# A Fourier mixer and a gated MLP in one kernel: who issues the first loads, and where z1's differences are kept

## The chip, the cores and the metric

The kernel runs on one core of a Trainium2 chip. The metric is the device time of one execution in microseconds (us). Each engine has a queue of its own that it works off in order: TensorE (PE) for matrix products, VectorE (DVE), ScalarE (ACT), GpSimd (POOL), and SyncE (SP), which here only issues DMA transfers. ACT and POOL can issue transfers too; such an issue, with whatever it waits for, stands in the engine's queue like any other instruction.

## The reference

```python
mod = (silu(c) @ w_mod).reshape(...)           # sa, ca, ga, sb, cb, gb
h = layernorm(x) * (1 + ca) + sa               # x: 2048 x 512, float32
a, b = h @ hid_re.T, h @ hid_im.T              # Fourier transform over 512 columns
x = x + ga * (seq_re @ a - seq_im @ b)         # and over 2048 rows, real part
h = layernorm(x) * (1 + cb) + sb
z = gelu(h @ w_in)                             # w_in: 512 x 1792
z1, z2 = z[:, :896], layernorm(z[:, 896:])
g = w_sp @ z2 + b_sp[:, None]                  # w_sp: 2048 x 2048
out = x + gb * ((z1 * g) @ w_out)
```

All of it is float32.

## The kernel before

Every product is made of three products of a shorter format. A matrix is split in a high part, which ScalarE makes by a copy into float32r, and a low part, which DVE makes as the difference (`split`). PE then adds high x high, high x low and low x high into the same bank of PSUM.

The program is written in one order by hand: a loop runs over steps n, each with its matrix products, and a table, filled by `at(n, function, arguments)`, says what else is issued at step n. No scheduler moves anything; every engine gets its instructions in the order in which the code calls them. Waits between engines are semaphores that the framework sets. A transfer issued by SP or ACT also gets one of eight semaphore lanes, DMAHW0 to DMAHW7, in turn by the order of the code, whichever of the two engines issues it, and it waits on its own engine's queue until the transfer before it on that lane has landed.

The first part (steps 0 to N2 - 1) forms the product of the sequence transform with the normalised x. The left operand's rows, 128 at a time, are x's (`hh` and `hl`, high and low part); the right operand comes from blocks of the transform's matrix: a block (`stage`) is loaded, turned in squares of 32 by DVE (`t`, L190), and split in `ah` (ACT, L289) and `al` (DVE, L307). The products of the first four steps use the same form (`mm_a`, L501): for a row s first `ah` with `hh`, then `al` with `hh`, then `ah` with `hl`.

Before the loop stands the head, code that brings the first four rows of x in by hand. `load_two` and `load_x` load a row of x in four transfers, `load_half` half of a stage in four. `stats_first` takes a row's mean and variance on DVE and the scale and shift from them on POOL (L427, L428). `hi_first` makes hh of a row straight from x on ACT (L444) and then writes ones into its first column (L446). `norm_x` makes the normalised row `xn` on ACT, after POOL has written its first column (L468); `hi_h` makes hh from xn (L477); `lo_h` makes hl from xn and hh on DVE (L482). `prep_hi` and `prep_lo` make t and ah, and al. `keep_busy` is eight products at the very start whose result nobody uses.

The second place is z1 = gelu(h @ w_in[:, :896]), from step N2 on, at about 455 us. It is computed by a scheme of seven products in place of eight (Strassen's, in Winograd's form; the products have numbers p, in the order of `YPROD`), which needs sums and differences of quarters of h and of w_in. For it DVE forms `vj`'s low part (`lo_v`) after ACT formed its high part (`hi_v`); the halves' differences `XD`, the sums `s` (L245) and, for the columns that do not fit the scheme (product `f7`), the high and low parts of the second halves of h (`make_x`, `xh` and `xl`). ACT empties the banks: z1o (L731, a gelu) and z1p (L759, a copy back into PSUM).

```python
YPROD = (1, 2, 6, 7, 4, 5, 3)
```

Of the kernel before, what the change touches and what calls it, by code (L numbers as in the profile page):

```python
# [8 lines left out]
F32 = mybir.dt.float32  # L9
F32R = mybir.dt.float32r  # L10
AF = mybir.ActivationFunctionType
ALU = mybir.AluOpType

P = 128
# [5 lines left out]
def fnet_gmlp_kernel(  # L20
# [32 lines left out]
    nc = tc.nc  # L53
    S, D = x.shape[1:]
    F2 = w_in.shape[1]
    FH = F2 // 2
    Q = 512
# [5 lines left out]
    x = x.rearrange("b s d -> (b s) d")  # L63
# [59 lines left out]
    def at(n, f, *a):  # L123
        fill.setdefault(n, []).append((f, a))
# [9 lines left out]
    src = []  # L134
# [4 lines left out]
    N2 = 4 * len(src)  # L139
    YPROD = (1, 2, 6, 7, 4, 5, 3)  # L140
# [9 lines left out]
    stage, T, AH, AL = {}, {}, {}, {}  # L150
# [6 lines left out]
    def load_half(tile_, a, h, engs=(nc.sync,) * 4):  # L157

        v = a.rearrange("(b j) (a s) -> a j b s", j=32, a=4)
        for q in range(4):  # L160
            engs[q].dma_start(tile_[32 * q:32 * q + 32], v[q][:, :, 64 * h:64 * h + 64])
# [39 lines left out]
    def slot(i, name, dtype=F32):  # L201
        return slots[0].tile([P, Q], dtype, tag=f"slot{i}", bufs=1, name=name)

    slots, TT, S2, XH = [], {}, {}, {}

    def load_t(g):
        for k in range(ND):
            TT[k, g] = slot(1 + 4 * (g - 2) + k, f"tt{g}_{k}")
            nc.sync.dma_start(TT[k, g], ht_d[g][k * P:(k + 1) * P, :])

    def make_x(gg):

        if gg:
            XH[gg] = [[bpool[0].tile([P, Q], F32R, tag=m, bufs=3, name=f"x{m}{kk}") for m in ("bh", "bl")] for kk in range(2)]
        else:
            XH[gg] = [(slot(9 + kk, f"xh{gg}{kk}", F32R), slot(11 + kk, f"xl{gg}{kk}", F32R)) for kk in range(2)]
        for kk, (h, _) in enumerate(XH[gg]):
            nc.scalar.activation(h, TT[kk, 2 + gg], AF.Copy)
        for kk, (h, l) in enumerate(XH[gg]):
            t = TT[kk, 2 + gg]  # L220
            nc.vector.tensor_tensor(l, t, h.bitcast(F32), op=ALU.subtract)
            if not gg:
                nc.vector.tensor_tensor(t, TT[kk, gg], t, op=ALU.subtract)
        if gg:
            for kk in range(2):
                TT[kk, 3] = XD[kk]

    XD = []

    def make_d():  # L230

        for kk in range(2):
            XD.append(bpool[0].tile([P, Q], F32, tag=("bh", "bl")[kk], bufs=3, name=f"xd{kk}"))
            nc.vector.tensor_tensor(XD[kk], TT[kk, 1], TT[kk, 3], op=ALU.subtract)

    def form_t(n):

        stage1 = n < N3
        p = (YPROD if stage1 else ZPROD)[(n - (N2 if stage1 else N3)) // 4]
        gg, kk = divmod(n % 4, 2)  # L240
        a, b, c, d = TT[kk, gg], TT[2 + kk, gg], TT.get((kk, 2 + gg)), TT.get((2 + kk, 2 + gg))
        if p == 6:
            if stage1:
                S2[gg, kk] = slot(13 + 2 * gg + kk, f"s2_{gg}{kk}")
                nc.vector.tensor_tensor(S2[gg, kk], d, XD[kk] if gg else c, op=ALU.subtract)  # L245
            return S2[gg, kk]
        if stage1:
            return {1: a, 2: b, 7: a, 4: b, 5: c, 3: d}[p]
        if p in (1, 2):
            t = blocks.tile([P, Q], F32, tag="t", bufs=2, name=f"t{n}")  # L250
            nc.vector.tensor_tensor(t, a if p == 1 else b, S2[gg, kk], op=ALU.subtract if p == 1 else ALU.add)
            return t
        return {7: c, 4: d, 5: a, 3: b}[p]
# [60 lines left out]
    spool = s1.enter_context(pool("spool", "right"))  # L314
# [91 lines left out]
    def load_x(g, ks=range(4), eng=nc.sync):  # L406

        if g not in XG:
            XG[g] = spool.tile([P, 4, D], F32, tag="x", bufs=2, name=f"x{g}")
        k0, k1 = ks[0], ks[-1] + 1  # L410
        v = x.rearrange("(g a k i) d -> g a i k d", g=NQ, a=4, i=32)
        for a in range(4):
            eng.dma_start(XG[g][32 * a:32 * a + 32, k0:k1, :], v[g, a][:, k0:k1, :])
        for k in ks:
            X[4 * g + k] = XG[g][:, k, :]
# [4 lines left out]
    def stats_first(s):  # L420

        m = spool.tile([P, 12], F32, tag="first", bufs=4, name=f"first{s}")
        nc.vector.bn_stats(m[:, :6], X[s])
        mv = m[:, 8:]
        nc.vector.bn_aggr(mv[:, :2], m[:, :6])
        nc.vector.tensor_scalar(mv[:, 1:2], mv[:, 1:2], EPS, None, op0=ALU.add)
        nc.gpsimd.tensor_tensor(mv[:, 2:3], mv[:, 1:2], mhalf, op=ALU.pow)  # L427
        nc.gpsimd.tensor_scalar(mv[:, 3:4], mv[:, 0:1], mv[:, 2:3], -1.0, op0=ALU.mult, op1=ALU.mult)  # L428
        NRM[s] = mv[:, 2:3], mv[:, 3:4]
# [1 line left out]
    two = (nc.sync, nc.sync, nc.scalar, nc.scalar)  # L431

    def load_two(k):
        if not k:
            XG[0] = spool.tile([P, 4, D], F32, tag="x", bufs=2, name="x0")
        v = x.rearrange("(g a k i) d -> g a i k d", g=NQ, a=4, i=32)
        for a in range(4):
            two[a].dma_start(XG[0][32 * a:32 * a + 32, k, :], v[0, a][:, k, :])
        X[k] = XG[0][:, k, :]

    def hi_first(s):
        h_hi[s] = hpool.tile([P, ND, P], F32R, name=f"hh{s}")
        h = h_hi[s].rearrange("p k (a i) -> p k a i", i=32)
        nc.scalar.activation(h, X[s].rearrange("p (a k i) -> p k a i", a=4, i=32), AF.Identity,  # L444
                             bias=NRM[s][1], scale=NRM[s][0])
        nc.scalar.activation(h_hi[s][:, 0, :1], ones[:, :1], AF.Copy)  # L446
# [16 lines left out]
    def norm_x(s):  # L463

        if s not in LN:
            LN[s] = spool.tile([P, D], F32, tag="xn", bufs=4, name=f"xn{s}")
        if s > 1:
            nc.gpsimd.memset(LN[s][:, 0:1], 1.0)  # L468
        apply(LN[s][:, 1:], X.pop(s)[:, 1:], NRM.pop(s))
# [5 lines left out]
    def hi_h(s):  # L475
        h_hi[s] = hpool.tile([P, ND, P], F32R, name=f"hh{s}")
        nc.scalar.activation(*parts_h(s, h_hi), AF.Copy)  # L477

    def lo_h(s):
        h_lo[s] = hpool.tile([P, ND, P], F32R, name=f"hl{s}")  # L480
        lo, h = parts_h(s, h_lo)
        nc.vector.tensor_tensor(lo, h, parts_h(s, h_hi)[0].bitcast(F32), op=ALU.subtract)  # L482
        LN.pop(s)
# [172 lines left out]
    def hi_v(p):  # L656
        WJ[1, p] = wpool[0].tile([P, 2, 2, Q], F32R, tag="wj", bufs=2, name=f"vj{p}")
        nc.scalar.activation(WJ[1, p][:, 0, :, :FM], v_of(p), AF.Copy)
# [56 lines left out]
    def end_f7(g):  # L715
        end_z1(g, NF - 1, ZT.pop(("f7", g)), out_row(g, NF - 1))
# [23 lines left out]
    def mm_z1(n):  # L740
        p = YPROD[(n - N2) // 4]
        gg = n % 4 // 2
        fresh = p in (1, 5)
        a = [(AH.pop(m), AL.pop(m)) for m in (n, n + 1)]
        if p in (2, 3):
            for kk, t in enumerate(a):
                mm_f7(gg if p == 2 else 2 + gg, 2 + kk, *t)
        for f in range(3):
            if fresh:
                ZT[gg, f] = bank(3 * gg + f, f"z1p{p}_{gg}{f}")  # L750
            cols = slice(f * P, (f + 1) * P)
            for kk, (th, tl) in enumerate(a):
                matmul3(ZT[gg, f], WJ[1, p][:, 0, kk, cols], WJ[1, p][:, 1, kk, cols], th, tl,
                        fresh and kk == 0, kk == 1, not fresh)
        ahead(n)
        for f in range(3):
            empty_z1(p, gg, f)
            if p == 2:
                nc.scalar.activation(turned(ZT[gg, f]), natural(Z1.pop((1, gg, f))), AF.Copy)  # L759
        if p == 1:  # L760
            for kk, t in enumerate(a):
                mm_f7(gg, kk, *t)
        if p == 2 and gg:
            hi_v(7)
            end_f7(1)

    def empty_z1(p, gg, f):
# [232 lines left out]
    load_two(0)  # L1000
    stage[0] = blocks.tile([P, 16, P], F32, tag="stage", bufs=2, name="stage0")
    load_half(stage[0][:, :, :64], src[0], 0, two)
    load_two(1)
    nc.scalar.activation(sc, ones[:, :ND], AF.Silu)
    load_x(0, range(2, 3))
    load_half(stage[0][:, :, 64:], src[0], 1)
    load_x(0, range(3, 4))
    load(1)
    load_x(1, range(2))
# [7 lines left out]
    stats_first(1)  # L1017
    prep_lo(0)
    norm_x(0)
    hi_first(1)  # L1020
    prep_hi(1)
    lo_h(0)
    stats_first(2)
    prep_lo(1)
    norm_x(1)
    lo_h(1)
    norm_x(2)
    hi_h(2)
    prep_hi(2)
    stats_first(3)  # L1030
    norm_x(3)
    at(0, lo_h, 2)
    at(0, hi_h, 3)
    at(1, lo_h, 3)
    at(0, load_x, 1, range(2, 4))
    at(2, load_row)
# [7 lines left out]
    for s, n in ((4, 4), (5, 4), (6, 6), (7, 6), (8, 10), (9, 10)):  # L1044
        m = n + (s == 9)
# [117 lines left out]
    at(N2 + 1, load_wi, 1, 2)  # L1163
    at(N2 + 2, form_v, 6)
    at(N2 + 3, load_t, 3)
    at(N2 + 4, make_x, 0)
    at(N2 + 6, make_d)
    at(N2 + 8, sum_x11, 0)
    at(N2 + 10, sum_x11, 1)
    at(N2 + 12, sum_x12, 0)  # L1170
    at(N2 + 14, sum_x12, 1)
    at(N2 + 13, form_v, 5)
    at(N2 + 17, form_v, 3)
    for i, p in enumerate(YPROD[2:]):
        if p != 7:
            at(N2 + 4 + 4 * i - (not i), hi_v, p)
        at(N2 + 5 + 4 * i - 2 * (not i), lo_v, p)
    at(N2 + 10, make_x, 1)
    at(N2 + 20, form_w, 7)
    at(NY[3], hi_w, 1)  # L1180
# [163 lines left out]
```

## Time and profile before

| | |
|---|---|
| median of three runs | 941.64 us (941.33 to 941.99) |
| the profiled execution | 941.69 us, of which the span of its instructions is 939.9 us |
| PE busy | 931.0 us, 99% of the span, 4112 matrix products |
| weight loads beside them | 771.6 us, 82% |
| DVE busy | 737.3 us, 78% |
| ACT busy | 414.3 us, 44% |
| POOL busy | 195.9 us, 21% |
| granted TensorE clock | 1.000 |
| DMA | 157.08 MB, 167 GB/s on average |

Busy shares are an average over the whole program. Where one engine is busy for 99% of the span, the remaining idle time of that engine, 939.9 - 931.0 = 8.9 us, is what work around it can save. The line numbers (L501) are those of the kernel before; in the kernel after the same lines stand some 7 or 8 lines earlier.

### The profile page before, as it was taken

The page shows a single profiled execution, that of the slowest core. Times are in us where ns is not written, and L with a number is a line of the kernel's source. Part 1 is how long each engine was busy: PE and PEld are TensorE (multiplying, and loading weights), DVE is VectorE, ACT ScalarE, POOL GpSimd, SP SyncE. Part 2 cuts the span into 40 slices and gives each one's busy share as a digit, 9 for nine tenths or more (in the row PEclk, how much of TensorE's full clock was granted, in tenths as well). Part 3 has the DMA queues.
Part 4 walks back from the last instruction along what each step waited for, and adds up shares of the span by engine and source line. Part 5 has one row for each costly group of instructions (what it writes and reads, how often), then busy time and mean ns, then how long its engine had stood idle before and what let it go on. Part 6 is the DMA issues. An engine that isn't in the chain of part 4 may idle for free.

```text
span 939.9 us, 12367 instructions
## 1 busy us (share of the span) xinstructions
PE 931.0 (99%) x4112; PEld 771.6 (82%) x4112; DVE 737.3 (78%) x1203; ACT 414.3 (44%) x728; POOL 195.9 (21%) x370
## 2 busy tenths in 40 slices
PE   8999999999999999999999999999999999999998
PEld 5888888888888888888878999888888888888886
DVE  6789957778677677875889878899799889886662
ACT  5685424232132222222488678674545544331221
POOL 2330000114554165323424211332000000000000
PEclk9999999999999999999999999999999999999999
DMA  9995762647539977994777523344564466744551
GB/s 204 226 224 123 144 145 68 168 135 183 141 86 303 294 212 215 277 336 147 234 279 271 183 92 74 92 100 104 130 140 107 114 145 135 179 112 145 183 176 56
DMA packets 236656, 157.08 MB, mean 167 GB/s; under 512 B 131536, under 2 KB 203472, under 8 KB 236464
## 3 DMA queue, kind: packets, MB, share of 16 engines
q1 hardware_dynamic: 222016, 118.39, 50.9%
q0 software_dynamic: 12128, 37.11, 11.0%
q10 hardware_dynamic: 2448, 0.79, 0.3%
q8 instruction: 32, 0.52, 0.2%
q14 instruction: 32, 0.26, 0.1%
HBM read 119.54 MB, written 36.70 MB: 166 GB/s over the span
## 4 chain that ended last, share of the span: by engine, by line
PE 92%; DVE 3%; ACT 2%; issue 1%; POOL 1%; DMA 0%; ACTq 0%; DVEq 0%; POOLq 0%
PE gp L96 12%; PE gp L97 12%; PE gp L95 12%; PE gw L95 10%; PE gw L96 10%; PE gw L97 10%; PE op L97 3%; PE op L96 3%; PE op L95 3%; PE yp L97 3%; PE yp L95 3%; PE yp L96 3%; PE z2p L96 2%; PE z2p L97 2%; PE z2p L95 2%; PE z1p L97 1%
## 5 line engine op out<-in xcount | busy, mean ns | idle before, releaser
L289 ACT ACTIVATE ah<-t 128x512 fp32r<-128x512 f32 x244 | 154.0, 632 | 370.3 <-DVE t L190 244.0
L307 DVE TENSOR_TENSOR al<-t,ah 128x512 fp32r<-128x512 f32 x244 | 164.0, 673 | 63.5 <-PE gp L96 37.5
L95 PE MATMUL gp<-ah,hh 128*128 128x512 f32 x496 | 193.0, 389 | 0.0
L97 PE MATMUL gp<-ah,hl 128*128 128x512 f32 x496 | 193.0, 389 | 0.0
L96 PE MATMUL gp<-al,hh 128*128 128x512 f32 x496 | 192.9, 389 | 0.0
L190 DVE STREAM_TRANSPOSE t<-stage 128x512 f32<-128x512 f32 x236 | 165.8, 702 | 10.4 <-DMA stage<-in_A_dft_seq_re_dram 4.0
L96 PE MATMUL gw<-al,bh 128*128 128x512 f32 x400 | 155.6, 389 | 0.0
L97 PE MATMUL gw<-ah,bl 128*128 128x512 f32 x384 | 149.5, 389 | 0.0
L95 PE MATMUL gw<-ah,bh 128*128 128x512 f32 x384 | 149.4, 389 | 0.0
L95 PEld LDWEIGHTS gp<-ah,hh 128*128 128x128 f32 x496 | 93.1, 188 | 19.4
L97 PEld LDWEIGHTS gp<-ah,hl 128*128 128x128 f32 x496 | 93.1, 188 | 19.3
L96 PEld LDWEIGHTS gp<-al,hh 128*128 128x128 f32 x496 | 93.1, 188 | 19.3
L96 PEld LDWEIGHTS gw<-al,bh 128*128 128x128 f32 x400 | 75.1, 188 | 15.5
L97 PEld LDWEIGHTS gw<-ah,bl 128*128 128x128 f32 x384 | 72.1, 188 | 15.3 <-DVE bl L874 0.3
L95 PEld LDWEIGHTS gw<-ah,bh 128*128 128x128 f32 x384 | 72.1, 188 | 15.0
L846 POOL DMA_DIRECT2D s_d<-sj x64 | 35.1, 548 | 99.0 <-DVE sj L838 73.9
L95 PE MATMUL yp<-hth,gh 128*128 128x512 f32 x128 | 49.8, 389 | 0.0
L96 PE MATMUL yp<-htl,gh 128*128 128x512 f32 x128 | 49.8, 389 | 0.0
L97 PE MATMUL yp<-hth,gl 128*128 128x512 f32 x128 | 49.8, 389 | 0.0
L623 POOL DMA_DIRECT2D ht_d<-hturn x62 | 40.9, 665 | 23.6 <-DVE hturn L619 19.6
L95 PE MATMUL op<-woh,uh 128*128 128x512 f32 x112 | 43.6, 389 | 0.0
L96 PE MATMUL op<-wol,uh 128*128 128x512 f32 x112 | 43.6, 389 | 0.0
(222 smaller groups left out, 1464.3 us busy)
## 6 DMA issues: line engine op xcount, KB each, us to landing
stage<-in_A_dft_seq_im_dram SPq DMA_DIRECT2D x64, 256.0 KB, 5.4
sj<-in_B_w_sp_dram SPq DMA_DIRECT2D x32, 512.0 KB, 7.6
s_d<-sj POOLq DMA_DIRECT2D x64, 256.0 KB, 4.1
stage<-s_d SPq DMA_DIRECT2D x128, 128.0 KB, 2.9
stage<-in_A_dft_seq_re_dram SPq DMA_DIRECT2D x60, 256.0 KB, 5.5
stage<-in_B_w_sp_dram SPq DMA_DIRECT2D x88, 128.0 KB, 3.2
wm<-in_w_mod_dram SPq DMA_DIRECT2D x16, 256.0 KB, 5.7
xr<-in_A_x_dram POOLq DMA_DIRECT2D x16, 256.0 KB, 4.2
```

The lines of the kernel that those rows point to most:

```text
L95: nc.tensor.matmul(acc, ah, bh, start=first, stop=False, skip_group_check=go_on)
L96: nc.tensor.matmul(acc, ah, bl, start=False, stop=False, skip_group_check=go_on)
L97: nc.tensor.matmul(acc, al, bh, start=False, stop=last, skip_group_check=go_on)
L190: nc.vector.transpose(dst.rearrange("p (b i) -> p b i", i=32), block[:, :, 32 * k:32 * k + 32])
L289: nc.scalar.activation(AH[n], T[n], AF.Copy)
L307: nc.vector.tensor_tensor(AL[n], t, AH[n].bitcast(F32), op=ALU.subtract)
L623: eng.dma_start(v[a, i], ht[32 * a:32 * a + 32].rearrange("c (b r) -> c b r", r=32))
L846: nc.gpsimd.dma_start(s_d[m, r, g][b * P:(b + 1) * P, :], a)
```

## The change

It has two parts that have nothing to do with each other.

In the head, the second half of the first stage was loaded by SP, after three rows of x; now ACT issues its four transfers, and they stand in ACT's queue ahead of the first hh. x's second row, of which ACT issued two transfers, is now SP's alone. On ACT, ah of a row now stands ahead of its hh (after the first row). hh of the third and fourth row is made straight from x (`hi_first`) where it was made from xn (`hi_h`). POOL writes the first columns of the third and fourth xn behind the statistics of all four rows.

In z1, the halves' differences get buffers of their own (slots 9 to 12), where they used to overwrite the halves, and are formed ahead of vj's low part. The high and low parts of both halves (`make_x`) use one kind of buffer, and the first of them come one step later, at N2 + 5 in place of N2 + 4.

```diff
 two = (nc.sync, nc.sync, nc.scalar, nc.scalar)
...
 load_two(0)
 stage[0] = blocks.tile([P, 16, P], F32, tag="stage", bufs=2, name="stage0")
 load_half(stage[0][:, :, :64], src[0], 0, two)
-load_two(1)
+load_x(0, range(1, 2))
 nc.scalar.activation(sc, ones[:, :ND], AF.Silu)
+load_half(stage[0][:, :, 64:], src[0], 1, (nc.scalar,) * 4)
 load_x(0, range(2, 3))
-load_half(stage[0][:, :, 64:], src[0], 1)
 load_x(0, range(3, 4))
...
 norm_x(0)
-hi_first(1)
 prep_hi(1)
 lo_h(0)
+hi_first(1)
 stats_first(2)
 prep_lo(1)
 norm_x(1)
+prep_hi(2)
 lo_h(1)
+hi_first(2)
+stats_first(3)
+prep_lo(2)
 norm_x(2)
-hi_h(2)
-prep_hi(2)
-stats_first(3)
+prep_hi(3)
+hi_first(3)
 norm_x(3)
 at(0, lo_h, 2)
-at(0, hi_h, 3)
```

```diff
+def make_d(gg):
+    for kk in range(2):
+        XD[gg, kk] = slot(9 + 2 * gg + kk, f"xd{gg}{kk}")
+        XR[gg, kk] = TT[kk, 2 + gg]
+        nc.vector.tensor_tensor(XD[gg, kk], TT[kk, gg], XR[gg, kk], op=ALU.subtract)
+        TT[kk, 2 + gg] = XD[gg, kk]
 def make_x(gg):
-    if gg: XH[gg] = ... bpool tiles bh, bl
-    else:  XH[gg] = ... slots 9 to 12
+    XH[gg] = ... bpool tiles bh, bl
     for kk, (h, _) in enumerate(XH[gg]):
-        nc.scalar.activation(h, TT[kk, 2 + gg], AF.Copy)
+        nc.scalar.activation(h, XR[gg, kk], AF.Copy)
...
-at(N2 + 4, make_x, 0)
-at(N2 + 6, make_d)
+at(N2 + 3, make_d, 0)
+at(N2 + 5, make_x, 0)
+at(N2 + 6, make_d, 1)
...
+at(N2 + 3, hi_v, 6)
+at(N2 + 4, lo_v, 6)
+at(N2 + 8, lo_v, 7)
```

(The table's entries for the other vj and the place of one emptying, `end_f7(1)`, which moves from step N2 + 6 to N2 + 8, are left out.)

ACT's queue at the start, before; in brackets stands what an instruction waits for, and the numbers behind the names tell tiles apart:

```order
L438 DMA x_129<-in_A_x_dram 32x512 x2
L161 DMA stage_134<-in_A_dft_seq_re_dram 32x16x64 x2
L438 DMA x_129<-in_A_x_dram 32x512 [waits DMAHW0_49]
L438 DMA x_129<-in_A_x_dram 32x512 [waits DMAHW2_49]
L1004 ACT_TABLE_LOAD
L1004 ACTIVATE sc<-ones 128x4 [waits Pool_49]
L444 ACTIVATE hh_181<-x_129,first_175 128x512 [waits DMAHW3_49,DMAHW1_49,Pool_49]
L446 ACTIVATE hh_181<-ones 128x1 [waits Activation_49]
L289 ACTIVATE ah_186<-t_184 128x512 [waits DVE_49]
```

The same after the change:

```order
L430 DMA x_129<-in_A_x_dram 32x512 x2
L161 DMA stage_134<-in_A_dft_seq_re_dram 32x16x64 x2
L997 ACT_TABLE_LOAD
L997 ACTIVATE sc<-ones 128x4 [waits Pool_49]
L161 DMA stage_134<-in_A_dft_seq_re_dram 32x16x64 [waits DMAHW2_49]
L161 DMA stage_134<-in_A_dft_seq_re_dram 32x16x64 [waits DMAHW7_49]
L161 DMA stage_134<-in_A_dft_seq_re_dram 32x16x64 [waits DMAHW4_49]
L161 DMA stage_134<-in_A_dft_seq_re_dram 32x16x64 [waits DMAHW0_49]
L436 ACTIVATE hh_181<-x_129,first_175 128x512 [waits DMAHW3_49,DMAHW1_49,Pool_49]
L438 ACTIVATE hh_181<-ones 128x1 [waits Activation_49]
L282 ACTIVATE ah_186<-t_184 128x512 [waits DVE_49]
```

Two transfers of x have gone, and four of the stage now stand between the write of sc and the first hh.

POOL's queue over the third and the fourth row (first_206 is the third row's statistics, xn_217 the third row's xn), before:

```order
L427 TENSOR_TENSOR first_206<-first_206,mhalf 128x1
L428 TENSOR_SCALAR first_206<-first_206 128x1
L468 MEMSET xn_217 128x1
L427 TENSOR_TENSOR first_226<-first_226,mhalf 128x1
L428 TENSOR_SCALAR first_226<-first_226 128x1
L468 MEMSET xn_232 128x1
```

and after, where the third row's xn is xn_232:

```order
L420 TENSOR_TENSOR first_206<-first_206,mhalf 128x1
L421 TENSOR_SCALAR first_206<-first_206 128x1
L420 TENSOR_TENSOR first_224<-first_224,mhalf 128x1
L421 TENSOR_SCALAR first_224<-first_224 128x1
L460 MEMSET xn_232 128x1
L460 MEMSET xn_247 128x1
```

The third row's memset has moved behind the two operations on the fourth row.

ACT's queue in z1, from vj's high part on (s_00 and s_01 are the first two sums; z_1 holds the first product's values), before:

```order
L658 ACTIVATE vj_4372<-w1e 128x2x384
L218 ACTIVATE xh_4375<-tt_0_4308 128x512
L218 ACTIVATE xh_4377<-tt_1_4310 128x512
L731 ACTIVATE z1o_6_4391<-f7p_4272 128x4x4x32
L289 ACTIVATE ah_4414<-s_00_4412 128x512
L289 ACTIVATE ah_4418<-s_01_4416 128x512
L731 ACTIVATE z1o_0_4420<-z1p_00_4241 128x4x4x32
L759 ACTIVATE z1p_00_4241<-z_1_00_4266 128x512
```

and after:

```order
L650 ACTIVATE vj_4378<-w1e 128x2x384
L723 ACTIVATE z1o_6_4387<-f7p_4274 128x4x4x32
L282 ACTIVATE ah_4410<-s_00_4408 128x512
L282 ACTIVATE ah_4414<-s_01_4412 128x512
L723 ACTIVATE z1o_0_4416<-z1p_00_4243 128x4x4x32
L751 ACTIVATE z1p_00_4243<-z_1_00_4268 128x512
L723 ACTIVATE z1o_1_4420<-z1p_01_4250 128x4x4x32
L751 ACTIVATE z1p_01_4250<-z_1_01_4270 128x512
L723 ACTIVATE z1o_2_4424<-z1p_02_4257 128x4x4x32
L751 ACTIVATE z1p_02_4257<-z_1_02_4272 128x512
L225 ACTIVATE xbh_4432<-tt_0_4310 128x512
L225 ACTIVATE xbh_4434<-tt_1_4312 128x512
```

The high parts of h's second halves (xh, now xbh) have moved from ahead of the sums' high parts to behind the emptying of three banks.

More of the change, by code (lines that the diff above doesn't have):

```diff
@@ L209, in load_t @@
             nc.sync.dma_start(TT[k, g], ht_d[g][k * P:(k + 1) * P, :])
+    XR, XD = {}, {}
+    def make_d(gg):
[4 more added lines that the diff above has]
+            TT[kk, 2 + gg] = XD[gg, kk]
     def make_x(gg):
[L213 to L216, printed above, removed]
+        XH[gg] = [[bpool[0].tile([P, Q], F32R, tag=m, bufs=3, name=f"x{m}{gg}{kk}") for m in ("bh", "bl")] for kk in range(2)]
         for kk, (h, _) in enumerate(XH[gg]):
-            nc.scalar.activation(h, TT[kk, 2 + gg], AF.Copy)
+            nc.scalar.activation(h, XR[gg, kk], AF.Copy)
         for kk, (h, l) in enumerate(XH[gg]):
[L220 to L234, printed above, removed]
+            nc.vector.tensor_tensor(l, XR[gg, kk], h.bitcast(F32), op=ALU.subtract)
     def form_t(n):
@@ L244, in form_t @@
                 S2[gg, kk] = slot(13 + 2 * gg + kk, f"s2_{gg}{kk}")
-                nc.vector.tensor_tensor(S2[gg, kk], d, XD[kk] if gg else c, op=ALU.subtract)
+                nc.vector.tensor_tensor(S2[gg, kk], d, c, op=ALU.subtract)
             return S2[gg, kk]
@@ L433, in load_two @@
     def load_two(k):
-        if not k:
-            XG[0] = spool.tile([P, 4, D], F32, tag="x", bufs=2, name="x0")
+        XG[0] = spool.tile([P, 4, D], F32, tag="x", bufs=2, name="x0")
         v = x.rearrange("(g a k i) d -> g a i k d", g=NQ, a=4, i=32)
@@ L764, in mm_z1 @@
             hi_v(7)
+        if n == N2 + 8:
             end_f7(1)
@@ L1173, in fnet_gmlp_kernel @@
     at(N2 + 17, form_v, 3)
[L1174 to L1177, printed above, removed]
+    at(N2 + 3, hi_v, 6)
+    at(N2 + 4, lo_v, 6)
+    at(N2 + 8, lo_v, 7)
+    for i, p in enumerate(YPROD[4:]):
+        at(N2 + 12 + 4 * i, hi_v, p)
+        at(N2 + 13 + 4 * i, lo_v, p)
     at(N2 + 10, make_x, 1)
```

## The prediction

> **What bounds the kernel now.** I read the chain of waits first, then the busy time by stretches, and then the two places that the change touches, row by row.
>
> ```profile
> PE 92%; DVE 3%; ACT 2%; issue 1%; POOL 1%; DMA 0%; ACTq 0%; DVEq 0%; POOLq 0%
> ```
>
> The chain that ended last is TensorE (PE) for 92% of the span. In the stretches (the first number after the length is TensorE's busy time, then its matmuls) one sees where it is not full:
>
> ```profile
> 21.10:455.00 433.90, 433.90 (x1916) 359.21 (x1915) 329.55 (x524) 156.72 (x276) 133.83 (x247) 1.00 0.75 194
> 455.00:500.00 45.00, 43.00 (x186) 34.31 (x185) 36.72 (x56) 32.44 (x61) 14.27 (x25) 1.00 0.64 226
> ```
>
> From 21.10 to 455 us 1916 matmuls fill 433.90 us, 0.2265 us each, with no gap. So the head counts only by the time at which this stretch begins. From 455 to 500 us 186 matmuls need 186 x 0.2265 = 42.13 us of 45.00, so 2.87 us are lost there. The change touches just these two places, and whatever it moves in either goes into the end time one for one.
>
> **The head: ScalarE's queue.** The timeline of ScalarE, and then of PE, at the start:
>
> ```profile
> 2.99 0.95 ACTq L438 DMA_DIRECT2D x<-in_A_x_dram  x2
> ...
> 6.00 0.81 ACT L444 ACTIVATE hh<-x,first 128x512 fp32r<-128x512 f32 x1 [0.53 <-POOL first L428]
> 6.84 0.20 ACT L446 ACTIVATE hh<-ones 128x1 fp32r<-128x1 f32 x1
> 6.95 0.61 ACT L289 ACTIVATE ah<-t 128x512 fp32r<-128x512 f32 x1
> ```
>
> ```profile
> 1.53 5.68 PE L389 MATMUL busyp<-busy,ones 128*128 128x512 f32 x8 [1.53 <-DVE busy L328]
> 7.62 1.20 PE L501 MATMUL gp<-ah,hh 128*128 128x512 f32 x4 [0.41 <-ACT ah L289]
> ```
>
> hh starts at 6.00, when the row's statistics come from GpSimd; hh, the write of ones and ah take 0.81, 0.20 and 0.61 us, and the first product follows 1.62 us after hh's start, at 7.62.
>
> After the change ScalarE no longer issues its two transfers of x's second row (0.95 us), and issues four of the stage's second half, ahead of hh in its queue. Each waits for the landing of an earlier transfer on its semaphore lane: an early x row, a first-half transfer of the stage, the fourth transfer of x's second row, and, for the fourth, the third transfer of x's third row on SyncE (the order shows lane DMAHW0 for it). hh, ready to go at 6.00, stands behind all four. So the question is when SyncE's third transfer of x's third row lands. From the chain of waits at that place:
>
> ```profile
> 2.12 3.57 DMA stage<-in_A_dft_seq_re_dram
> ```
>
> SyncE's own timeline, start and length of its issues:
>
> ```profile
> 2.80 0.90 SPq L438 DMA_DIRECT2D x<-in_A_x_dram  x2
> 4.75 1.75 SPq L413 DMA_DIRECT2D x<-in_A_x_dram  x4
> ```
>
> The DMA view, for issues at 2.7 to 2.9 us and at 5.65 to 6.05 us (KB, us from issue to landing):
>
> ```profile
> x<-in_A_x_dram SPq DMA_DIRECT2D x1, 64.0 KB, 3.1
> ```
>
> ```profile
> x<-in_A_x_dram SPq DMA_DIRECT2D x1, 64.0 KB, 2.1
> ```
>
> The row of the chain is ScalarE's last first-half transfer: it lands at 5.69. SyncE's second transfer of x's third row waits for it on its lane, and takes 1.75 / 4 = 0.44 us to issue at most. The third also needs lane DMAHW0, whose last user is the first transfer of x's second row: issued at about 2.80 and 3.1 us under way (first row of the DMA view), it lands at 5.9. So the third goes out at about 6.1. Transfers issued around 5.9 took 2.1 us (its second row), which gives 8.2. ScalarE's fourth issue then takes 0.95 / 2 = 0.48 us at most, 0.4 taken: hh starts at 8.6 instead of 6.00, 2.6 us later, and the first product comes at 8.6 + 1.62 = 10.22.
>
> **From the first product to the full stretch.** Before, this took longer than the work needs. The chain of waits has the last of it:
>
> ```profile
> 18.27 3.01 PE gp L501 x12
> ```
>
> GpSimd's two operations on a row's statistics, the second one for x's first row, then both for its fourth:
>
> ```profile
> 5.69 0.27 POOL L428 TENSOR_SCALAR first<-first 128x1 f32<-128x1 f32 x1
> ...
> 14.57 0.55 POOL L427 TENSOR_TENSOR first<-first,mhalf 128x1 f32<-128x1 f32 x1 [2.38 <-DVE first L426]
> 15.22 1.11 POOL L428 TENSOR_SCALAR first<-first 128x1 f32<-128x1 f32 x1
> ```
>
> DVE's groups up to 17 us (busy time, mean ns of one, idle before):
>
> ```profile
> L190 DVE STREAM_TRANSPOSE t<-stage 128x512 f32<-128x512 f32 x4 | 2.8, 706 | 1.0 <-DMA stage<-in_A_dft_seq_re_dram 1.0
> L423 DVE BATCH_NORM_STATS2 first<-x 128x6 f32<-128x512 f32 x4 | 2.7, 682 | 2.6 <-DMA x<-in_A_x_dram 2.6
> L482 DVE TENSOR_TENSOR hl<-xn,hh 128x512 fp32r<-128x512 f32 x3 | 2.0, 675 | 0.1
> L307 DVE TENSOR_TENSOR al<-t,ah 128x512 fp32r<-128x512 f32 x3 | 2.0, 674 | 0.8 <-ACT ah L289 0.8
> L425 DVE BATCH_NORM_AGGREGATE first<-first 128x2 f32<-128x6 f32 x4 | 0.7, 182 | 0.1
> L426 DVE TENSOR_SCALAR first<-first 128x1 f32<-128x1 f32 x4 | 0.6, 153 | 0.1
> ```
>
> The fourth row's products start at 18.27 and end at 21.28, where the full stretch starts. The four rows have 4 x 12 = 48 matmuls, 48 x 0.2265 = 10.87 us; from 7.62 to 21.28 are 13.66, so 2.8 us of waits lay between the products before. The last of them is due to a chain: the fourth row's statistics, GpSimd's two operations (14.57 to 16.33), xn, and hh from xn. After the change hh of the third and fourth row comes straight from x, for 0.81 + 0.20 us, without xn ahead of it; ScalarE has room for that beside PE's work (if not, it costs 0.4 per row). That shortens the chain, and so the later start eats these waits first.
>
> What comes last then is the low part of the third row, hl. In the new order GpSimd sets the first element of that row's xn behind both operations of the fourth row, and hl needs it. DVE gets from ah's end (10.22) to the fourth row's statistics by two each of al, t, hl and statistics: 2 x (0.674 + 0.706 + 0.675 + 0.682 + 0.182 + 0.153) = 6.14, less 0.3 since neighbours overlap by up to 0.09 (on ScalarE ah starts at 6.95, before 6.84 + 0.20): 16.0. GpSimd: 0.55, a step of 0.1, its second operation (1.11 in that row, 0.27 for the first row of x at 5.69; I take 0.75, nearer to the row of the same place, and keep both as bounds), 0.1 for the memset: 17.5. hl 0.68 and a step of 0.1: 18.3. Four matmuls of the third row and twelve of the fourth are left, 16 x 0.2265 = 3.62, and 0.1 for refilling the array after a wait: the full stretch starts at 22.0 instead of 21.28, **+0.7 us**. Bounds: with hl in time PE alone would be there at 10.22 + 10.87 + 0.4 = 21.5 (+0.2). With GpSimd at 1.11, and its first operation and the lane each 0.4 later, it is 23.1 (+1.8).
>
> SyncE loses four transfers and gains two of 0.44 us, so the next stage's go out about 1 us sooner. Nobody gains by it: with the new start DVE reaches that stage's blocks later than before.
>
> **The second place, z1.** The timelines of PE, of ScalarE and of DVE:
>
> ```profile
> 469.95 0.39 PE L95 MATMUL f7p<-xh,w 128*128 128x512 f32 x1
> ...
> 472.24 0.50 PE L95 MATMUL z1p<-ah,vj 128*128 128x512 f32 x1 [0.77 <-ACT z1p L759]
> ```
>
> ```profile
> 464.62 0.85 ACT L658 ACTIVATE vj<-w1e 128x768 fp32r<-128x768 f32 x1
> 465.35 1.16 ACT L218 ACTIVATE xh<-tt 128x512 fp32r<-128x512 f32 x2
> ...
> 469.83 1.23 ACT L289 ACTIVATE ah<-s 128x512 fp32r<-128x512 f32 x2 [2.83 <-DVE s L245]
> ...
> 473.89 0.60 ACT L759 ACTIVATE z1p<-z 128x512 f32<-128x512 f32 x1
> ```
>
> ```profile
> 465.50 0.96 DVE L662 TENSOR_TENSOR vj<-w1e,vj 128x768 fp32r<-128x768 f32 x1 [1.42 <-ACT vj L658]
> ...
> 469.04 1.28 DVE L245 TENSOR_TENSOR s<-tt,tt 128x512 f32<-128x512 f32 x2
> ```
>
> Before, DVE makes xl and the differences (4 operations) between vj and s, so s starts at 469.04 and ah at 469.83. Emptying the first bank follows on ScalarE, and PE, done with six matmuls of f7p at 469.95 + 6 x 0.2265 = 471.31, waits for that until 472.24. After the change the differences stand ahead of vj on DVE, where it waited 1.42 us anyway, and xl stands behind. s starts right after vj, at 466.4, and ScalarE's ah at 467.15, 2.7 us sooner. I take it that this removes the wait before 472.24 and those behind it, which stand on the same two queues: the whole 2.87.
>
> But xh moves too. It stood ahead of ah<-s (465.35) and is now behind ah<-s and the six operations that empty three banks (z1o and z1p). In the rows these take from 469.83 to 473.89 + 0.60 = 474.49, 4.66 us. From 467.15 that gives 471.8 for the start of xh, and 0.6 later, 472.4, for the first of its two halves. The f7 product of xh keeps its place on PE, and PE reaches it at 469.95: it waits 472.4 - 469.95 = 2.45 us. xl needs xh, 0.68 on DVE: another 0.5 until the second matmul, and 0.1 of refill. Sum 3.05. Behind it all is ready by then, so PE runs on. ScalarE and DVE come out of this about 1 us later than before, and one later row is near its limit:
>
> ```profile
> 499.07 0.95 DVE L662 TENSOR_TENSOR vj<-w,vj 128x768 fp32r<-128x768 f32 x1
> ```
>
> ```profile
> 500.81 0.39 PE L97 MATMUL z1p<-ah,vj 128*128 128x512 f32 x1
> ```
>
> vj's low part ends at 500.02, its user starts at 500.81: 0.79 us of slack against 1.1 to 1.3 of delay, 0.3 to 0.5 lost. z1 loses 3.05 + 0.4 = 3.45 in place of 2.87: **+0.6 us**, with bounds of 0 (the emptying 0.6 faster) and +0.9.
>
> **The sum.** The profiled execution took 941.69, 0.05 above the median of 941.64. 941.69 + 0.7 + 0.6 = 942.99, **943.0 us**. A measurement of this kernel tells a difference of about 0.2%, 1.9 us, from no change: 943.0 lies inside it.
>
> **The rivals.**
>
> R1, the clock: PE idles from the end of its eight warm-up matmuls, 1.53 + 5.68 = 7.21, to 10.22, which is 3.0 us where it was 0.41, and comes back at a lower clock. No row of this kernel shows a gap of that length. At half rate for as long as the warm-up took, 5.68 us, 2.8 us would be lost; half of that, less what the wait for hl hides, is +1.3, and gives 944.3: slower. It decides from the point where the idle stretch is long enough for the throttle. The Trainium skill, "TensorE: Matmul & The Clock Gate", section "What's actually happening", has the array fall to half rate after an idle window of about 3.4 us, in windows that run freely; by that rule 3.0 us would just not do it, and 0.4 us more of waiting could; no run here shows it yet. Chance 0.12.
>
> R2, the lanes run later: x's third row takes 3.1 us (as the earlier row of the DMA view) and not 2.1, and hh starts at 9.6. Everything from DVE's chain on moves with it, +1.0, and GpSimd at its 1.11 adds 0.3: 943.0 + 1.3 = 944.3, slower. For it: the stage's second half now travels beside x's third row, where it used to follow it. Against: the bytes are the same in all. Chance 0.20.
>
> R3, the queue isn't held: ScalarE's four issues pass early, hh starts at about 6.5, the full stretch at 6.5 + 1.62 + 10.87 + 1.0 = 20.0, -1.3: 941.69 - 1.3 + 0.6 = 941.0. Against it: every lane has a user before. For it: the times of the landings are worked out, not seen. Chance 0.08.
>
> R4, z1's waits all go: were xh ready by 469.95, the whole 2.87 would be won: 941.69 + 0.7 - 2.87 = 939.5, faster. Against: the order has xh behind the emptying of the banks, which itself needs 4.66 us. Chance 0.05.
>
> **How the numbers follow.** The forecast has the remaining 0.55; its own range is 941.9 to 944.0 (head +0.2 to +1.4, z1 0 to +0.9), and 0.08 of the 0.55 lies above 941.64 + 1.88 = 943.5, where slower begins. Slower: 0.12 + 0.20 + 0.08 = 0.40. Same: the other 0.47 and R3's 0.08, 0.55. Faster: 0.05. The range reaches over R1 and R2, with 0.5 for their own spread, and below the forecast's own range to just above R3: 941.2 to 944.8. R3, R4 and the far ends of R1 and R2 are left out.
>
> **What would show it.** Right: hh's idle time on ScalarE ended by DMA issues, hh at 8 to 9 us, first product at 10 to 10.5, the full stretch from about 22; f7p's first matmul on xbh waiting for ScalarE by 2.4 us, no wait at the products behind it, a small one near 501. Wrong: hh before 7, a PE clock under 1.00 in the first 20 us, f7p's wait gone, or another wait of over 1 us anywhere.

## The result, and the profile after

The changed kernel takes 945.19 us (median of five, 945.11 to 945.30) against 941.64: a ratio of 1.0038, 95% interval 1.0023 to 1.0052. It is slower by 3.55 us, and 945.19 lies 0.4 us above the range. The profiled execution took 945.30, its span is 943.5 against 939.9, and its mean granted clock is 0.996 against 1.000. In two of the experiments one execution (1912.26 us with z1 alone, 1249.12 us with the longer warm-up) is far slower than all others of its kernel, and the ratios leave it out.

The same two stretches as before, shifted by 2.4 us since the full stretch begins that much later (columns as in the prediction; the third number from the end is the granted TensorE clock):

```profile
23.50:457.40 433.90, 433.90 (x1916) 359.32 (x1915) 329.48 (x522) 156.13 (x276) 135.27 (x247) 1.00 0.74 192
457.40:502.40 45.00, 42.75 (x181) 34.64 (x180) 35.97 (x56) 32.46 (x60) 13.50 (x24) 0.96 0.66 223
```

The full stretch is the same, 1916 matmuls in 433.90 us. Its first product, before and then after:

```profile
21.12 0.39 PE L95 MATMUL gp<-ah,hh 128*128 128x512 f32 x1
```

```profile
23.52 0.39 PE L95 MATMUL gp<-ah,hh 128*128 128x512 f32 x1
```

It starts 2.4 us later. In z1 181 matmuls fit in 45 us, where 186 did: 5 x 0.2265 = 1.1 us more. So 2.4 us went in the head and 1.1 to 1.2 in z1, and both together are the 3.6 us of the span.

ScalarE's timeline in the head:

```profile
3.52 0.32 ACTq L161 DMA_DIRECT2D stage<-in_A_dft_seq_re_dram  x1
4.00 0.20 ACT L997 ACTIVATE sc<-ones 128x4 f32<-128x4 f32 x1
5.27 3.87 ACTq L161 DMA_DIRECT2D stage<-in_A_dft_seq_re_dram  x3
9.27 0.81 ACT L436 ACTIVATE hh<-x,first 128x512 fp32r<-128x512 f32 x1 [5.07 <-DMA x<-in_A_x_dram]
```

The four issues hold the queue until 9.14, and hh, which started at 6.00 before, starts at 9.27. The chain of waits names the last of what they waited for:

```profile
6.12 2.68 DMA x<-in_A_x_dram
8.80 0.02 issue
8.82 0.32 ACTq L161
```

That is the transfer of x's third row that the prediction named, out at 6.12 and landed at 8.80. PE, and the same time in stretches of 3.4 us:

```profile
1.53 5.62 PE L382 MATMUL busyp<-busy,ones 128*128 128x512 f32 x8 [1.53 <-DVE busy L321]
10.89 1.20 PE L493 MATMUL gp<-ah,hh 128*128 128x512 f32 x4 [3.74 <-ACT ah L282]
```

```profile
6.80:10.20 3.40, 0.35 (x1) 0.00 (x0) 1.03 (x3) 0.90 (x2) 0.82 (x2) 1.00 0.78 206
10.20:13.60 3.40, 2.71 (x9) 2.19 (x10) 2.67 (x5) 2.69 (x6) 0.00 (x0) 0.81 1.02 237
13.60:17.00 3.40, 3.40 (x12) 2.66 (x12) 3.32 (x8) 2.82 (x6) 2.01 (x3) 0.69 1.18 234
17.00:20.40 3.40, 3.40 (x17) 2.82 (x16) 2.87 (x6) 2.95 (x6) 0.93 (x4) 1.00 0.55 149
```

After 3.74 us of idle time the granted clock is 0.81 and then 0.69. In the third of these rows PE is busy throughout, yet has 12 matmuls, where the fourth has 17. Cut where the clock changes, the low clock lasts 3.41 us and is half of the full one; the two rows ahead of it show how much TensorE did before:

```profile
5.46:8.87 3.41, 1.69 (x4) 0.38 (x2) 1.74 (x4) 0.00 (x0) 0.39 (x3) 1.00 0.86 214
8.87:12.28 3.41, 1.39 (x6) 1.17 (x7) 1.41 (x3) 2.31 (x5) 0.74 (x2) 1.00 0.87 227
12.28:15.69 3.41, 3.41 (x10) 2.63 (x9) 3.34 (x8) 2.83 (x6) 1.69 (x2) 0.50 1.21 229
```

The chain shows all 48 products of the first four rows without a wait, in 12.79 us:

```profile
10.89 12.79 PE gp L493 x48
```

The last of them ends at 23.68, 0.16 us after the next product has started. From the first start, 10.89, to that next start, 23.52, are 12.63 us; at full clock 48 products take 10.87, so the low clock costs 1.76 us there.

z1: PE's waits, and the chain of waits just behind them:

```profile
PE f7p L95 <- ACT xbh L225: 2.0, 1, 2.0
PE f7p L96 <- DVE xbl L227: 0.2, 1, 0.2
```

```profile
476.22 0.23 PE f7p L96
476.45 0.28 PE f7p L97
476.73 0.43 PE z1p L95
...
479.29 0.43 PE z1p L95
479.72 0.38 PE z1p L96
480.10 0.23 PE z1p L97
```

The only waits left are those for xbh and xbl, as forecast. But from 476.5 to 479.9, 3.4 us, a matmul takes 0.43 instead of 0.23: about eight at half clock, 8 x 0.2 = 1.6 us that stood in no term of the sum. The stretches show the same drop, behind one in which TensorE was busy for about half:

```profile
473.08:476.49 3.41, 1.74 (x6) 1.23 (x7) 1.98 (x4) 1.89 (x4) 0.54 (x1) 1.00 0.90 222
476.50:479.91 3.41, 3.41 (x9) 2.63 (x8) 3.26 (x6) 2.18 (x4) 0.20 (x1) 0.50 1.02 401
```

### The profile page after: what moved, and what is told of

Same layout as the page of the kernel before. It is cut to its first block, busy times and chain, and to the rows that moved or that the text cites. A ratio compares the mean times of both kernels' runs of the same rounds, so it can differ in the third digit from the quotient of the medians.

```text
span 943.5 us, 12369 instructions
## 1 busy us (share of the span) xinstructions
PE 932.2 (99%) x4112; PEld 774.7 (82%) x4112; DVE 738.8 (78%) x1203; ACT 414.8 (44%) x730; POOL 195.5 (21%) x370
## 4 chain that ended last, share of the span: by engine, by line
PE 94%; DVE 2%; ACT 1%; DMA 1%; POOL 1%; issue 1%; ACTq 0%; SPq 0%; DVEq 0%; POOLq 0%
PE gp L97 12%; PE gp L95 12%; PE gp L96 12%; PE gw L95 10%; PE gw L97 10%; PE gw L96 10%; PE op L97 3%; PE op L96 3%; PE op L95 3%; PE yp L96 2%; PE yp L97 2%; PE yp L95 2%; PE z2p L96 2%; PE z2p L97 2%; PE z2p L95 2%; PE z1p L95 2%
## 5 line engine op out<-in xcount | busy, mean ns | idle before, releaser
L95 PEld LDWEIGHTS gp<-ah,hh 128*128 128x128 f32 x496 | 93.1, 188 | 19.4
```

Of the source, the lines that this page charges most:

```text
L95: nc.tensor.matmul(acc, ah, bh, start=first, stop=False, skip_group_check=go_on)
```

## The experiments

Theory A: the first hh stands behind the second half's transfers on ScalarE, f7p behind xbh; and TensorE, little used for a few us, then runs at half clock for about 3.4 us, in both places. Its rivals say that the low clock comes from something else, or that another part of the reordering costs the time.

**The head alone.** The head as changed, z1 as before.

> The head of the change with z1 as before. In the profile after, the full stretch begins 2.4 us later than before (23.5 against 21.1), 1.9 us of that with TensorE at a granted clock of 0.81 and 0.69 between 10 and 17 us. Theory A (the queue is held and then the clock drops, and the two parts of the change simply add): 941.64 + 2.4 = 944.0, same low clock in the head, none later. Rival (the low clock comes of the run as a whole, not of the head's gap): the low clock also stands in z1, and the time is nearer to 945.

Measured: 944.76 us (943.37 to 945.31), ratio 1.0027 (1.0016 to 1.0038). In its profile z1's clock is 1.00 and PE waits there at before's three places (0.7, 0.5 and 0.4 us, where before had 0.7, 0.5 and 0.8). The head has the low clock, for longer than in the changed kernel's profile:

```profile
10.20:13.60 3.40, 2.56 (x6) 2.08 (x7) 2.54 (x5) 2.69 (x6) 0.00 (x0) 0.50 1.05 236
13.60:17.00 3.40, 3.40 (x10) 2.64 (x10) 3.29 (x9) 2.73 (x7) 1.94 (x3) 0.57 1.17 243
```

With the clock at 0.50 and 0.57, that is over 5 us of half clock: the 48 products take 13.57 us from 11.04 to 24.61, 2.7 more than at full clock. So the price of the drop differs between runs, which would account for their spread of 1.9 us and for the 0.8 us by which 944.0 was missed: the three runs with a mean clock of 0.996 took 944.77 to 945.31, the four with 0.998 took 943.37 to 944.76. The rival, a low clock of the run as a whole, falls, though the median lies nearer to its 945 than to 944.0.

**z1 alone.** The head as before, z1 as changed.

> z1 of the change with the head as before. Theory A (TensorE waits 2.2 and 0.5 us for xbh and xbl in f7p, and is then at half clock for 3.4 us since it was idle, which costs 1.6 to 1.7): z1 loses 4.4 to 4.5 us where it lost 3.0, 943.1. Rival (the low clock in z1 is an after-effect of the head's): the wait stays, the low clock goes, z1 loses 2.8 to 3.0, 941.6.

Measured: a median of 942.48, ratio 1.0008 (0.9999 to 1.0017), between the two expectations. But the runs fall in two groups. Four took 943.06 to 944.06, each with a granted clock of 0.998; six took 941.76 to 942.48 with 0.999 or 1.0. The profiled one is of the first group (PE's waits, and the stretch behind them):

```profile
PE f7p L95 <- ACT xbh L225: 2.2, 1, 2.2
PE f7p L96 <- DVE xbl L227: 0.2, 1, 0.2
```

```profile
472.00:482.00 10.00, 9.24 (x32) 7.29 (x33) 7.05 (x11) 7.20 (x13) 1.76 (x4) 0.83 1.01 313
```

The low clock is there without the head's, so the rival (an after-effect) falls. That the same program gets it in some runs and not in others neither theory had said. It would fit a window on a beat of its own, which cuts the 2.7 us of idle time in two or not: in the changed kernel's profile the two slow stretches of 3.41 us begin at 12.28 and 476.50, 464.22 us apart, which is 136 times 3.413. Runs without a profile don't show where their windows lay, so this stays open.

**The second half issued by SyncE.** The changed kernel, with one thing undone:

```diff
-load_half(stage[0][:, :, 64:], src[0], 1, (nc.scalar,) * 4)
+load_half(stage[0][:, :, 64:], src[0], 1)
```

> The changed kernel with one thing undone: the second half's four transfers are issued by SyncE, at the same place of the code. Theory A (the first hh stands behind these transfers' waits on ScalarE): hh at 6.0, first product at 7.6, no low clock in the head, the full stretch at about 19.4, z1 as in the changed kernel: 945.2 - 4.1 = 941.1. Rival (it is the other order of the head, or the transfers side by side, that cost the time): first product after 9, 943 or more.

Measured: 942.71 us (941.49 to 943.68), ratio 1.0007 (0.9998 to 1.0016), 1.6 us above what was expected. Here too the mean clock differs between runs: six with 0.998 took 942.45 to 943.68, five with 0.999 or 1.0 took 941.49 to 942.71. The queue is free, as expected: hh starts when its statistics are there,

```profile
5.94 0.81 ACT L436 ACTIVATE hh<-x,first 128x512 fp32r<-128x512 f32 x1 [1.74 <-POOL first L421]
```

the first product comes at 7.61, and the head's clock is 1.00. But the full stretch starts at 21.57, not at 19.4. The chain of waits and then DVE and PE tell why:

```profile
12.29 5.88 DMA stage<-in_A_dft_seq_im_dram
```

```profile
18.29 0.71 DVE L190 STREAM_TRANSPOSE t<-stage 128x512 f32<-128x512 f32 x1 [1.52 <-DMA stage<-in_A_dft_seq_im_dram]
```

```profile
19.63 1.19 PE L493 MATMUL gp<-al,hh 128*128 128x512 f32 x4 [0.69 <-DVE al L300]
```

With all transfers on SyncE the next stage lands at 18.16, and its first t stands ahead of the fourth row's al in DVE's queue: a new wait in place of the old. So the held queue is shown, and so is that freeing it alone gains nothing in the head against before, whose full stretch starts at 21.12.

**A longer warm-up.** The changed kernel with

```diff
-keep_busy(4, 5)
+keep_busy(7, 5)
```

> The changed kernel with seven warm-up products in place of four, so that TensorE is busy until 9.7 instead of 7.1 and then idle for 1.2 us. Theory A (a window of about 3.4 us in which TensorE is busy for less than about half makes the next one run at half clock): first product still at 10.9, granted clock 1.00 in the whole head, the full stretch at 21.9 to 22.4 instead of 23.5, since the low part of the third row then waits 0.5: 944.0 to 944.4 if z1 is unchanged. Rival (the low clock stands for another reason, as the load of the DMA engines): clock and time as before, 945.2.

Measured: 943.98 us, ratio 1.0020 (1.0010 to 1.0030), just at the lower end of what was expected. PE's timeline, and the stretches:

```profile
10.87 1.20 PE L493 MATMUL gp<-ah,hh 128*128 128x512 f32 x4 [0.77 <-ACT ah L282]
```

```profile
10.20:13.60 3.40, 2.73 (x12) 2.11 (x13) 2.68 (x6) 2.69 (x6) 0.00 (x0) 1.00 1.00 234
13.60:17.00 3.40, 3.40 (x16) 2.59 (x15) 3.33 (x8) 2.82 (x6) 2.02 (x3) 1.00 1.16 230
...
472.00:482.00 10.00, 8.41 (x29) 6.63 (x30) 6.23 (x11) 7.17 (x14) 2.16 (x4) 0.83 0.99 328
```

The first product is as late as in the changed kernel, the transfers are the same, and the clock in the head is 1.00: it was the idle time. In z1, where nothing was changed, the clock still falls, behind waits of 1.8 and 0.2 us. It does not in every run: six with a mean clock of 0.998 took 943.80 to 944.14, three with 0.999 or 1.0 took 942.88 to 943.25.

**Products in z1's wait.** z1 alone as above, and in `mm_x`, ahead of f7p's first product on xbh, nine products into the bank that it starts anew:

```diff
+if gg == 0:
+    ps = bank(6, "busyz")
+    for _ in range(9):
+        nc.tensor.matmul(ps, W7[0][:, 0, 0], W7[0][:, 0].rearrange("p k q -> p (k q)"), start=True, stop=True)
```

> Head as before, z1 as changed, and nine extra products ahead of f7p's xbh products, into the bank that these start anew, so that TensorE is busy for 2.0 us of the 2.3 that it waits. Their result is not used. Theory A (a window of 3.4 us with little work makes the next one slow): f7p's first product at the same time, granted clock at 1.00 in z1, 1.6 us less than the runs with the low clock, 941.6 to 942.2 in all runs. Rival (the low clock has another cause than the idle time): 943.2 in part of the runs as without the extra products.

Measured: 941.96 us, ratio 1.0004 (0.9995 to 1.0013). All eleven runs have a clock of 0.999 or 1.0; nine lie within the expected interval, two above it (942.31 and 942.92). The upper one is the profiled run: its first product in the head came at 8.10 instead of 7.62, which has nothing to do with z1. The group of 943 with the low clock is gone. One reservation: z1 alone ran on another chip, where before took 941.75 us and not 941.67, and it was not run again on this one.

**Both.** The changed kernel with the longer warm-up and the nine products.

> The changed kernel with seven warm-up products in place of four and the nine extra products in z1: TensorE idles for no longer than 1.2 us anywhere. Theory A: clock 1.00 throughout, and what is left is the late start and the waits themselves: head +1.0, z1 0 to +0.1, 942.6 to 942.9, against 945.2 of the changed kernel. Rival (the clock is only part of it, or drops elsewhere): 943.5 or more.

Measured: 942.82 us (942.64 to 943.04), ratio 1.0013 (1.0004 to 1.0022), as expected. All eleven runs have a clock of 0.999 or 1.0. Against the changed kernel's 945.19 the low clock is worth 2.4 us; it is less than 1.76 + 1.6, since at full clock waits appear that the slow products had covered. The 1.15 us that are left against before's 941.67 stand for the held queue and the waits at full clock: its full stretch starts at 22.39, 1.27 us later than before.

**xbh ahead.** The head as before, z1 as changed, with the high parts back in their place and the low parts where the change has them:

```diff
-at(N2 + 5, make_x, 0)
+at(N2 + 4, make_x, 0)
+at(N2 + 5, make_xl, 0)
```

(`make_x(0)` makes xbh alone here; the new function `make_xl` makes xbl.)

> Head as before, z1 as changed but for one thing: the high parts xbh stand where they stood before the change, right behind vj's high part on ScalarE; xbl keeps its changed place. Theory A (the whole loss of the changed z1 is xbh's place behind the emptying of three banks, and the clock that follows from the wait): no wait at f7p, the sums 2.6 us earlier than before, no low clock, most of the 3.0 us of before's waits gone: 939.0 to 939.6. Rival (the bank emptying or the differences' place is what TensorE waits for): the wait turns up at the next product, 941 or more.

Measured: 938.68 us (938.58 to 939.45), ratio 0.9970 (0.9959 to 0.9981), 0.3 us better than expected. ScalarE's timeline and z1's stretch:

```profile
464.94 1.15 ACT L225 ACTIVATE xbh<-tt 128x512 fp32r<-128x512 f32 x2
465.98 0.60 ACT L729 ACTIVATE z1o<-f7p 128x512 f32<-128x512 f32 x1
466.76 1.24 ACT L287 ACTIVATE ah<-s 128x512 fp32r<-128x512 f32 x2 [0.18 <-DVE s L243]
```

```profile
455.00:500.00 45.00, 45.00 (x199) 36.81 (x198) 38.94 (x60) 35.43 (x65) 15.39 (x28) 1.00 0.69 240
```

ah<-s starts at 466.76 in spite of xbh ahead of it, and z1 has no gap: 45.00 us busy, 199 matmuls. The rest of z1's change (the differences in own buffers and earlier, and the entries moved with them) is worth 3.0 us; the place of xbh alone gave all of it back, also in those runs of z1 alone that kept the full clock (941.76 to 942.48). What each part of the rest gives was not taken apart.

**A version that beats both.** z1 as in the last run; in the head the second half by SyncE behind x's third row, and on DVE the second row's al ahead of the third row's statistics, the fourth row's al and hl ahead of the next stage's t:

```diff
-load_half(stage[0][:, :, 64:], src[0], 1, (nc.scalar,) * 4)
 load_x(0, range(2, 3))
+load_half(stage[0][:, :, 64:], src[0], 1)
...
 hi_first(1)
+prep_lo(1)
 stats_first(2)
-prep_lo(1)
...
 at(0, lo_h, 2)
-at(1, lo_h, 3)
+at(0, prep_lo, 3)
+at(0, lo_h, 3)
```

(Against the changed kernel; z1's two lines are those of the last run.)

> A version meant to beat both: z1 as in the run with xbh ahead; in the head the second half goes by SyncE behind x's third row, al of the second row ahead of the third row's statistics, al and hl of the fourth row ahead of the next stage's first block on DVE. Theory A: first product at 7.6, no low clock, the full stretch at 20.0 to 20.6 (before 21.1), z1 without waits: 938.0 to 938.8. Rival (the next stage lands too late, after 18.5, and holds the start back): the full stretch at 21.0 or later, 939.2 or more.

Measured: 937.56 us (937.52 to 937.66), ratio 0.9957 (0.9944 to 0.9969), 4.1 us less than before and 7.6 less than the changed kernel, a little below the expected interval.

```profile
19.78 0.39 PE L95 MATMUL gp<-ah,hh 128*128 128x512 f32 x1
20.28 0.50 PE L96 MATMUL gp<-al,hh 128*128 128x512 f32 x1
```

The full stretch starts at 19.78 with one wait of 0.3 us behind it. Which of the three edits of the head gives how much of the 1.1 us was not taken apart.

## Why the prediction was wrong

The bound and the places were right: TensorE sets the time, the 433.90 us between are unchanged, and both losses stand one for one in the result. So were the two mechanisms, the queue that the lanes hold and f7p's wait for xbh behind the emptying of three banks. Of the rivals R3 and R4 fell. What failed, in its terms:

- **The clock in the head, R1, was a rival with 0.12, and it happened.** It was priced at +1.3, stood outside the sum, and cost 1.76. Its sign, a clock under 1.00 in the first 20 us, is there. The idle stretch was taken at 3.0 us, and no row of before showed one of that length; it was 3.74. The Trainium skill, "TensorE: Matmul & The Clock Gate", "What's actually happening", has half rate after an idle window of about 3.4 us, and full rate again after a busy one of that length. The lengths of the slow stretches, 3.41 us in the head and in z1, agree with these figures. The stretch ahead of the head's drop does not: of the 3.41 us from 8.87 to 12.28 TensorE was busy for 1.39.
- **The clock in z1 stood in no term: 1.6 us.** The prediction asked for the clock only at the head, and took z1's wait of 2.45 + 0.5 as two gaps to be added up. Here too the rule of the Trainium skill, read as a window without any work, does not agree with the runs: the clock fell behind waits of 2.0 and 0.2, and 1.8 and 0.2 us, with TensorE at work inside the same 3.4 us. The measurement decides: a stretch of little use is enough. How little is not shown: 1.74 us of work in 3.41 were followed by half clock in z1, 1.69 in the head (5.46 to 8.87) were not.
- **The transfer: 2.1 taken, 2.68 measured.** It moved hh from 8.6 to 9.27 and the first product from 10.22 to 10.89. This is R2's mechanism at half its price.
- **The low part hl of the third row: 0.5 expected, none seen,** since the slow products came to it later. With the clock at 1.00 (both places kept busy) there are 0.25 us of wait at 18.58, so the mechanism was right and its size was half of what was taken.
- **z1 at full clock: +0.6 expected, about 0.3 or less seen.** The first wait was 2.2 (2.45 taken) and the second 0.5 by the starts of the products, as taken; the later one at vj near 501, 0.4 in the sum, did not come back, and the runs of z1 alone at a clock of 0.999 or more lie at 941.76 to 942.48, in the middle 942.0, against 941.75 for before on the same chip.

One slip is in the sum itself: it counts the head's loss from 21.28, where the last product before the full stretch ends, but the stretch starts at 21.12. From there to the forecast's 22.0 are 0.9 and not 0.7.

Added up: head 0.9 + 0.67 (transfer) + 1.76 (clock) - 0.9 (waits expected between the products, none seen) = 2.4; z1 0.6 - 0.3 (first wait) - 0.4 (vj) + 1.6 (clock) = 1.5. That gives 941.7 + 3.9 = 945.6, against 945.3 profiled; the 0.3 between lies in z1, whose losses the stretches show only in whole matmuls of 0.23.

One sentence ahead of the prediction is not right either: the lanes are not dealt by the order of the code alone. ScalarE's fourth transfer stands ahead of x's third row in the code, and waits for that row's third transfer on the same lane. The rows that show the waits (the order with its DMAHW numbers) were what the prediction went by, so this did no harm.

## What to carry to other kernels

A wait of a TensorE-bound kernel can cost more than its own length: here waits of 1.8 us and more cost 1.6 to 2.7 us on top where the clock fell to half behind them, so ask of every new wait, not only of the first one, how much work lies in the few us around it. Filling such a wait with products that nobody reads brought the clock back, and better still was to remove the wait. A transfer issued from an engine that computes puts its lane's wait ahead of that engine's work; read from the order which landing each issue waits for. Where an edit moves one thing forward, look at what it moved behind something else: z1's other edits were worth 3.0 us, and xbh's new place cost them all.

## What was not expected of the hardware

- The clock falls without a stretch that is wholly idle: waits of 1.8 and 0.2 us were enough, and in the changed kernel TensorE was busy for 1.39 and 1.74 of the 3.41 us ahead of the drops. The slow stretch then lasts 3.41 us, with about eight products of 0.43 in place of 0.23 us.
- The same wait in the same program brings the low clock in some runs and not in others (z1 alone: four runs at 943.06 to 944.06 and six at 941.76 to 942.48), and in one profile (the head alone) it lasted over 5 us. A median over such runs mixes two times; the clock beside each run tells them apart.
